# Starting the kv matmuls of batches 3 and 4 one schedule slot later in a fused attention and MLP kernel

## The chip, the cores and the metric

The kernel runs on one core of one Trainium2 chip. The metric is device time in microseconds (us) of the whole program. Executions of a kernel on this core differ by some tenths of a us, sometimes by more than one. Names used below: PE is the tensor engine, PEld its weight loads, DVE the vector engine, ACT the scalar engine, POOL the engine that issues the loads, SP the engine whose queue issues the DMA transposes and the output stores.

## The reference, cut to what matters

```python
def _attn_ref(q, k, v, g_norm):                      # q, k, v: (8, 8, 576, 64)
    kv = np.einsum('bhsd,bhse->bhde', k, v)          # one 64x64 matrix per batch and head
    out = np.einsum('bhsd,bhde->bhse', q, kv)
    rms = np.sqrt(np.mean(out * out, axis=-1, keepdims=True) + 1e-06)
    return out / rms * g_norm

def _moe_ref(x, g_ln, w_ch1, w_ch2):                 # x: (8, 576, 512)
    xn = (x - mean) / sqrt(var + 1e-06) * g_ln
    return x + np.maximum(xn @ w_ch1, 0.0) @ w_ch2   # 512 -> 2048 -> 512
```

## The kernel before

The MLP is the long part: for each batch, `mm1` (x to 2048 columns) and `mm2` (back to 512). The attention of later batches is interleaved with it by hand. A counter ticks once per group of four 512-column matmuls of the MLP (or the same number of columns in smaller pieces), 0.87 us; one such group is a *slot*. `at(slot, fn)` puts a piece of attention at a slot, and within a slot the pieces are emitted in the order of their fractional slot numbers. In the traces each engine runs its own instructions in the order emitted (in e4, e6 and e8 below, the one piece of DVE work whose slot is moved is the one that changes places there).

```python
    def load_batch(b, *after):
        for element in after:
            nc.gpsimd.tensor_copy(gate, element)      # POOL waits here until `element` exists
        load(k_in[b % NB], k, b)
        load(v_in[b % NB], v, b)
        load(q_in[b % NB], q, b)

    def kv_of(b):
        kv_ps = ps_m.tile([128, HP, D], f32, tag="misc", name="kv_ps")
        kvp = held[b] = kv_pack[b % 4]
        ...                                           # 40 matmuls kv_ps <- k_in, v_in
        nc.scalar.copy(kvp[:D, :, :D], kv_ps[:D])
        nc.scalar.copy(kvp[D:, :, D:], kv_ps[D:])

    def turn_q_dma(b):
        q_p = kv_in.tile([128, JJ, H, D], bf16, tag="qp", bufs=2)
        nc.vector.tensor_copy(q_p.rearrange("p j h d -> p h j d"), q_in[b % NB])
        q_t = qt_pool.tile([128, JJ, HP, 128], bf16, tag="qt", name="qt")
        nc.sync.dma_start_transpose(...)              # qt <- q_p, on SP's queue
        qts[b] = q_t
```

A tile of 128 tokens then goes through `o` (PE: qt times kv), a chain of norms on ACT and DVE that ends in `xc`, and a DMA transpose on SP's queue into `xT_blk`, which `mm1` reads. The schedule of batches 3 and up, with the parts that matter here:

```python
    for b in range(3, B):
        s = 32 * b                                    # slot at which mm1 of batch b starts
        at(47 if b == 3 else s - 60,
           lambda b=b: load_batch(b, qts[b - 1][...], ...))
        d = -41 if b == 3 else -45
        at(s + d, lambda b=b: kv_of(b))               # slot 55 for batch 3, slot 83 for batch 4
        at(s + d + 1.7, lambda b=b: turn_q_dma(b))    # 56.7 and 84.7
        for j in range(J):
            o = s + d + (11 if b == 3 else 13) + 5 * j
            plan_tile(o, lambda b=b, j=j: main_tile(b, j), o + 6, False)
        if b % 2:
            plan_tile(s - 14, lambda b=b: rem_tile(b), s - 8, False)
```

`plan_tile(o, ...)` puts the tile's first half (`o`, squares, sums) at slot `o`, its second half (`y`, `x`, `xc` on DVE) at `o + 2`, the variance at `o + 6`, and the DMA transpose at the slot given as the third argument (`o + 6` too for a tile of a batch). The first `o` of batch 3 is at slot 66, that of batch 4 at slot 96. `mm1` of batch 3 starts at slot 96 too, right after that `o`.

## Time and profile before

| | before |
|---|---|
| median of 4 runs | 290.67 us (290.46 to 290.76) |
| span of the profiled execution | 289.9 us |
| PE busy, granted clock | 96%, 0.997 |

Two parts of the page: the busy time of each engine, and the chain of work that ended last, by engine.

```profile
PE 278.9 (96%) x2270; PEld 158.1 (55%) x2295; DVE 149.8 (52%) x331; ACT 153.0 (53%) x333; POOL 41.2 (14%) x69
...
PE 69%; DMA 19%; issue 9%; POOL 2%; DVE 0%; POOLq 0%
```

PE has no free time to speak of, so only a gap on PE can be gained. (The Trainium skill, Perfetto Trace Analysis, section "Identifying the Most-Contended Engine", warns that matmul busy time is not a good measure of the distance to the peak, since matmuls are pipelined. It is used here only to say that PE seldom waits.) There were 2295 weight loads but 2270 matmul records: 25 records are missing.

Of the chain's 19% DMA, the page puts 14% down to the v_in loads. The three waits of PE that are longest in total (us in total, number, longest):

```profile
PE even L225 <- DMA v_in<-in_v_dram: 2.0, 1, 2.0
PE p L198 <- DVE eps_sb L137: 1.2, 1, 1.2
PE kv_ps L246 <- DMA v_in<-in_v_dram: 1.0, 2, 0.6
```

The first two are the start of the program. The third is the kv matmuls waiting for their v. The timeline of PE (start, duration, what; in brackets the idle time before it and what ended it) places them:

```profile
73.14 0.82 PE L246 MATMUL kv_ps<-v_in,k_in 128*64 128x64 bf16 x40 [0.39 <-DMA v_in<-in_v_dram]
74.12 0.59 PE L429 MATMUL p<-w_sb,m 128*128 128x512 bf16 x2 [0.16 <-issue]
...
101.03 0.82 PE L246 MATMUL kv_ps<-v_in,k_in 128*64 128x64 bf16 x40 [0.61 <-DMA v_in<-in_v_dram]
102.00 0.38 PE L429 MATMUL p<-w_sb,m 128*128 128x512 bf16 x1 [0.16 <-issue]
...
113.01 0.39 PE L271 MATMUL o_ps<-kv_pack,qt 128*128 128x128 bf16 x4
113.28 0.59 PE L413 MATMUL p<-xT_blk,w_sb 128*128 128x512 bf16 x2
```

The first lines of the pairs are kv of batch 3 and of batch 4. The last two lines are the first `o` of batch 4 and the first matmul of `mm1` of batch 3; that matmul needs the last xT transpose of batch 3. The timeline of SP's queue shows when it was issued:

```profile
107.51 3.14 SPq L205 DMA_TRANSPOSE qt<-q_p  x1
110.70 1.26 SPq L352 DMA_TRANSPOSE xT_blk<-xc  x1
```

By its semaphore it landed near 113.15, so `mm1` at 113.28 was already on its heels, without a visible wait. In front of it in the queue stands the q transpose of batch 4.

### The profile page before, as it was taken

The numbers are of one execution on the slowest core, as the hardware profiler recorded it, in microseconds if no ns is written. First come the engines' busy times: TensorE is split into PE (matmuls) and PEld (weight loads), VectorE is DVE, ScalarE is ACT, GpSimd is POOL, SyncE is SP. The second block draws the span as 40 slices with busy tenths as digits, with TensorE's granted clock in tenths as the row PEclk, the third lists the DMA queues.
The fourth block names the chain that finished last, engine by engine and source line by source line (L and its number), as shares of the span: only waits on it lengthen the run. The fifth ranks groups of instructions, "written<-read, shape, count | busy, mean of one in ns | idle before, by whom it ended". The sixth has DMA issues, their size and how long they took to land.

```text
span 289.9 us, 5728 instructions
## 1 busy us (share of the span) xinstructions
PE 278.9 (96%) x2270; PEld 158.1 (55%) x2295; DVE 149.8 (52%) x331; ACT 153.0 (53%) x333; POOL 41.2 (14%) x69
## 2 busy tenths in 40 slices
PE   8789999999999999999999999999999999999994
PEld 3579755995479644445444444444444444444444
DVE  5675119937897783765366925762578200220022
ACT  3467844985369732882288418920894076016400
POOL 8432510041006003200500032000000000000000
PEclk9999999999999999999999999999999999999998
DMA  7999999969786959996994189937202410230033
GB/s 213 198 206 203 199 177 193 221 109 192 138 171 98 198 100 169 196 162 110 158 221 77 39 148 215 156 79 158 55 18 58 107 36 0 45 83 20 0 74 74
DMA packets 67546, 36.76 MB, mean 127 GB/s; under 512 B 35516, under 2 KB 62524, under 8 KB 67520
## 3 DMA queue, kind: packets, MB, share of 16 engines
q0 software_dynamic: 28528, 17.76, 43.6%
q1 hardware_dynamic: 38480, 17.91, 30.3%
q10 hardware_dynamic: 512, 0.72, 0.7%
q8 instruction: 18, 0.29, 0.4%
q14 instruction: 8, 0.07, 0.1%
HBM read 36.71 MB, written 9.44 MB: 159 GB/s over the span
## 4 chain that ended last, share of the span: by engine, by line
PE 69%; DMA 19%; issue 9%; POOL 2%; DVE 0%; POOLq 0%
PE p L429 35%; PE p L413 31%; DMA v_in<-in_v_dram 14%; DMA w_sb<-in_moe_w_ch_dram 5%; PE o_ps L271 2%; PE kv_ps L246 1%; POOL k_in L93 0%; POOL v_in L93 0%; POOL k_in L94 0%; POOL q_in L94 0%; DVE o_sb L434 0%; POOL gate L98 0%; POOLq L93 0%; POOLq L94 0%; POOLq L690 0%
## 5 line engine op out<-in xcount | busy, mean ns | idle before, releaser
L413 PE MATMUL p<-xT_blk,w_sb 128*128 128x128 bf16 (+2 forms) x1017 | 131.3, 285 | 0.8
L429 PE MATMUL p<-w_sb,m 128*128 128x512 bf16 (+2 forms) x591 | 126.6, 368 | 1.5 <-issue 1.0
L416 ACT ACTIVATE m<-p 128x512 bf16<-128x512 f32 x144 | 85.4, 595 | 42.8 <-PE p L413 40.4
L413 PEld LDWEIGHTS <-w_sb 128*128 128x128 bf16 x1024 | 78.7, 98 | 44.5 <-issue 1.1
L429 PEld LDWEIGHTS <-m 128*128 128x128 bf16 x608 | 57.0, 98 | 62.1
L434 DVE SCALAR_TENSOR_TENSOR o_sb<-p,rstd,x_blk 128x512 f32<-128x512 f32 (+2 forms) x38 | 27.3, 720 | 52.9 <-PE p L429 47.3
L277 ACT ACTIVATE sq<-o_ps 128x512 f32<-128x512 f32 x35 | 20.9, 596 | 43.5 <-PE o_ps L271 43.5
L298 DVE TENSOR_REDUCE ss<-sq 128x8 f32<-128x512 f32 x35 | 23.7, 679 | 12.8 <-ACT sq L277 12.6
L340 ACT ACTIVATE dev<-x_blk,st_blk 128x512 f32<-128x512 f32 x36 | 25.7, 714 | 5.7 <-DVE st_blk L326 5.7
L332 DVE SCALAR_TENSOR_TENSOR xc<-x_blk,st_blk,g_ln_sb 128x512 bf16<-128x512 f32 x34 | 25.6, 752 | 1.2
L303 DVE TENSOR_TENSOR y<-o_ps,inv 128x512 f32<-128x512 f32 x33 | 22.8, 692 | 3.4 <-PE p L413 0.5
L322 DVE SCALAR_TENSOR_TENSOR x_blk<-y,g_norm_sb 128x512 f32<-128x512 f32 x33 | 22.8, 691 | 1.1
L315 DVE RECIPROCAL inv<-rms 128x8 f32<-128x8 f32 x36 | 7.2, 201 | 22.9 <-ACT rms L308 22.9
L422 DVE RECIPROCAL rstd<-rstd 128x4 f32<-128x4 f32 x9 | 1.6, 175 | 32.1 <-ACT rstd L421 32.0
L308 ACT ACTIVATE rms<-ss,eps_sb 128x8 f32<-128x8 f32 x36 | 10.7, 296 | 10.6 <-DVE ss L298 10.4
L98 POOL COPY gate<-qt 1x1 bf16<-1x1 bf16 x5 | 0.9, 178 | 106.8 <-DMA qt<-q_p 106.8
L271 PEld LDWEIGHTS <-qt 128*128 128x128 bf16 (+1 forms) x156 | 10.3, 100 | 7.5 <-issue 1.7
L271 PE MATMUL o_ps<-kv_pack,qt 128*128 128x128 bf16 (+1 forms) x156 | 13.6, 220 | 0.0
L198 PE MATMUL p<-fill_sb 128*128 128x512 bf16 x26 | 8.1, 461 | 1.3 <-DVE eps_sb L137 1.2
L246 PEld LDWEIGHTS <-k_in 128*64 128x64 bf16 x280 | 5.0, 112 | 3.7 <-issue 3.6
L249 ACT CAST kv_pack<-kv_ps 64x256 bf16<-64x256 f32 x7 | 2.5, 364 | 8.1 <-PE kv_ps L246 8.1
L340 ACT ACTIVATION_READ_ACCUMULATOR dev<-x_blk,st_blk 128x1 f32 x36 | 6.8, 189 | 0.0
(80 smaller groups left out, 110.9 us busy)
## 6 DMA issues: line engine op xcount, KB each, us to landing
out_dram<-o_sb SPq DMA_DIRECT2D x70, 128.0 KB, 2.5
w_sb<-in_moe_w_ch_dram POOLq DMA_DIRECT2D x8, 512.0 KB, 14.7
q_in<-in_q_dram POOLq DMA_DIRECT2D x7, 320.0 KB, 12.1
k_in<-in_k_dram POOLq DMA_DIRECT2D x7, 320.0 KB, 5.8
v_in<-in_v_dram POOLq DMA_DIRECT2D x7, 320.0 KB, 8.6
q_in<-in_q_dram POOLq DMA_DIRECT2D x8, 256.0 KB, 12.0
k_in<-in_k_dram POOLq DMA_DIRECT2D x7, 256.0 KB, 6.7
v_in<-in_v_dram POOLq DMA_DIRECT2D x7, 256.0 KB, 10.0
```

Source lines behind the costliest of these rows:

```text
L271: nc.tensor.matmul(flat[rows, hp * 128:(hp + 1) * 128], lhsT=lhsT_of(hp), rhs=kvp[:, hp, :], start=True, stop=True)
L277: nc.scalar.activation(self.sq_t, self.o_ps, func=AF.Square)
L298: nc.vector.tensor_reduce(self.ss, self.sq_t, axis=AX.X, op=ALU.add)
L303: nc.vector.tensor_mul(self.y_t, self.o_ps, self.inv().to_broadcast([128, H, D]))
L308: nc.scalar.activation(self.r, self.ss, func=AF.Sqrt, scale=1.0 / D, bias=eps_sb)
L322: nc.vector.scalar_tensor_tensor(x_blk[:, ts].rearrange("p (h d) -> p h d", h=H), in0=self.y_t, scalar=1.0, in1=g_norm_sb.to_broadcast([12 ...
L332: nc.vector.scalar_tensor_tensor(self.xc_t, in0=x_blk[:, self.ts], scalar=st[:, 1, self.ts:self.ts + 1], in1=g_ln_sb, op0=ALU.add, op1=ALU ...
L340: nc.scalar.activation(dev, x_blk[:, ts], func=AF.Square, bias=st[:, 1, ts:ts + 1], accum_out=st[:, 2, ts:ts + 1])
L413: nc.tensor.matmul(p1[:, i, :], lhsT=w1_sb[:, kk, de * 128:(de + 1) * 128], rhs=blk[2][:, kk, sl], start=(kk == 0), stop=(kk == nK - 1))
L416: nc.scalar.activation(m1[:, de0:de0 + per, sl], p1, func=AF.Relu)
L429: nc.tensor.matmul(p2[:, c0:c1], lhsT=m1s[b][:, de, ts * 128:(ts + 1) * 128], rhs=w2_sb[:, de, c0:c1], start=(de == 0), stop=(de == nDe - 1))
L434: nc.vector.scalar_tensor_tensor(o_sb[:, c0:c1], in0=p2[:, c0:c1], scalar=rstds[b][:, ts:ts + 1], in1=blks[b][0][:, ts, c0:c1], op0=ALU.mu ...
```

## The change

The intent is to let v land before PE comes to the kv matmuls: they move behind one more slot of MLP matmuls, and PE does that work in the time in which it waited.

```diff
-        at(s + d, lambda b=b: kv_of(b))
+        at(s + d + (1 if b < 5 else 0), lambda b=b: kv_of(b))
```

## The prediction

> **What bounds the kernel.** The tensor engine: the page has PE busy 96% of the 289.9 us span at a granted clock of 0.997, with 69% of the chain that ended last. In the waits of PE, the only wait on data in mid-kernel is kv_ps (the kv matmuls, L246) on the v_in load: 1.0 us, twice. The timeline of PE places them: kv of batch 3 starts at 73.14 after 0.39 us idle, kv of batch 4 at 101.03 after 0.61. kv of batch 5 (130.45) waits for nothing.
>
> **What the change does.** It adds and removes nothing. The 40 kv matmuls of batches 3 and 4, with their two casts on ACT, move behind one more slot of four 512-column matmuls (0.87 us in the timeline). turn_q_dma still comes right after kv, so VectorE and the DMA queue keep their order. The new kv is first used ten slots later.
>
> **Gain at the two places.** From the end of the matmul before to the next one after, an undisturbed kv (batch 5) takes 0.91 us. Batch 3 takes 72.75 to 74.12 = 1.37, batch 4 100.42 to 102.00 = 1.58. So 0.46 and up to 0.67 us can go. v_in of batch 3 landed at 72.96; kv would now start near 73.6: wait gone. v_in of batch 4 landed near 100.85; its load was gated at 89.10 by the last xT transpose of batch 2, which hangs on a VectorE chain that is back to back from 74 to 82, so I don't expect it earlier. PE would reach that kv near 100.42 - 0.46 + 0.87 = 100.83: at most 0.2 us of wait is left. PE is then 0.9 to 1.1 us ahead.
>
> **What takes part of it back.** The first mm1 matmul of batch 3 (113.28) needs all four xT tiles. The last transpose is issued at 110.70 and, by its semaphore, lands near 113.15: that matmul already starts on its heels. (The issue bar ends at 111.96; that the data movement lies outside it is what the Trainium skill, Perfetto Trace Analysis, section "DMA Instruction — HWDGE (DVE, Sync)", says, and this landing agrees.) If PE is 0.9 us early, it waits here, except as far as the transpose comes earlier too. Its chain backwards: qt transpose on the same queue (107.51 to 110.65), q_p copy on VectorE (106.63), VectorE back to back since 96.57, ACT rstd (96.25), ACT back to back since an eviction that waited for PE at 93.47. So it moves with PE as it stands before slot 83: by batch 3's 0.46 us, not by batch 4's gain. PE should get a new wait of about 0.4 us there, and the net gain is about 0.46 us. From there PE is the limit to the end (v_in of batch 5 has 6 us of margin).
>
> **Prediction.** 290.73 - 0.46, say 290.25 us; 8 times in 10 within 289.65 to 290.85. Faster by over 2%: 0.005; within 2%: 0.99; slower by over 2%: 0.005.
>
> **What would show it.** PE's waits: kv_ps on v_in gone or under 0.3 us in total. A new wait of PE at L413 near 112.8, of 0.3 to 0.6 us, released by the xT transpose. rstd on ACT near 95.8, last xT transpose of batch 3 issued near 110.2. kv of batch 5 near 130.0.
>
> **What would make it wrong.** The transpose's chain moves by the full 0.9 us (gain near 1.0), or not at all since ACT or VectorE hold it (gain near 0.05). The load gate of batch 4 shifts, and v_in with it by some tenths. A new buffer wait in mm2 of batch 1, whose last p2 bank has about 0.6 us of margin.

## The result

The time did not move: 290.70 us median (290.36 to 291.18, 4 runs) against 290.67 us, ratio 1.0003, 95% interval 0.9986 to 1.002. (A ratio is the mean time of one kernel's fast runs over that of the other's fast runs of the same rounds, so it is not quite the ratio of the medians.)

The profile after, the page's busy line and all waits of PE:

```profile
PE 282.2 (98%) x2295; PEld 158.1 (55%) x2295; DVE 149.8 (52%) x331; ACT 153.3 (53%) x333; POOL 40.9 (14%) x69
```

```profile
PE p L198 <- DVE eps_sb L137: 1.2, 1, 1.2
PE even L225 <- DMA v_in<-in_v_dram: 0.4, 1, 0.4
PE tp L554 <- DVE xc L547: 0.4, 1, 0.4
PE p L413 <- DMA xT_blk<-xc: 0.2, 1, 0.2
PE kv_ps L246 <- issue: 0.2, 1, 0.2
```

The wait of kv on v_in is gone, and `mm1` waits for the xT transpose. The start of the program also waited 1.6 us less for its first v, by chance. Do not read "PE 98%" as a gain: 25 more matmuls have a record here. The lines of the PE timeline that answer to those before:

```profile
73.11 0.82 PE L246 MATMUL kv_ps<-v_in,k_in 128*64 128x64 bf16 x40
...
100.53 0.82 PE L246 MATMUL kv_ps<-v_in,k_in 128*64 128x64 bf16 x40
...
112.56 1.24 PE L413 MATMUL p<-xT_blk,w_sb 128*128 128x512 bf16 x5 [0.24 <-DMA xT_blk<-xc]
```

Two more waits hide in the weight loads. In the timeline of PEld (the first line is `o` of batch 3, the second `o` of batch 4, both of their first tile):

```profile
83.40 0.23 PEld L271 LDWEIGHTS <-qt 128*128 128x128 bf16 x4 [0.32 <-DMA qt<-q_p]
...
111.92 0.23 PEld L271 LDWEIGHTS <-qt 128*128 128x128 bf16 x4 [0.59 <-DMA qt<-q_p]
```

The view of PE's own waits does not list these two: qt is the weight operand, so the wait belongs to the weight load, and PE's pause in that time lies under the modelled end of the matmul before it. SP's queue after:

```profile
106.83 3.09 SPq L205 DMA_TRANSPOSE qt<-q_p  x1
109.98 1.26 SPq L352 DMA_TRANSPOSE xT_blk<-xc  x1
```

**A measure without the start-up.** From the first matmul to the first kv matmul of batch 2 the profiled executions of all kernels here took 51.7 to 52.7 us, although nothing there was changed. From the first kv matmul of batch 5 to the end they took 159.39 to 159.43 us. So the stretch between, *kv of batch 2 to kv of batch 5*, holds all that the change does: 76.50 us before, 76.20 us after. Times in the rest of the text are counted from the first kv matmul of batch 2.

In that stretch I took, at five places, the distance between the starts of two successive matmuls, less the distance usual at that place (0.31 us in front of kv; 0.11 and 0.22 in front of the first `o` of batches 3 and 4; 0.06 between that `o` and `mm1`). That is the wait there, free of modelled ends. "Sum" is their total, "rest" the stretch less the sum. The table has all runs, those of the next section too.

| run | kv b3 on v_in | o b3 on qt | kv b4 on v_in | o b4 on qt | mm1 b3 on xT | sum | stretch | rest |
|---|---|---|---|---|---|---|---|---|
| before | 0.45 | 0 | 0.68 | 0 | 0.05 | 1.18 | 76.50 | 75.32 |
| after | 0 | 0.20 | 0 | 0.26 | 0.40 | 0.86 | 76.20 | 75.34 |
| e1_after_again | 0 | 0.23 | 0.08 | 0.16 | 0.46 | 0.93 | 76.28 | 75.35 |
| e2_only_batch3 | 0 | 0.20 | 0.62 | 0 | 0.05 | 0.86 | 76.19 | 75.33 |
| e3_only_batch4 | 1.15 | 0 | 0 | 0.26 | 0.40 | 1.81 | 77.14 | 75.33 |
| e4_q4_early | 0 | 0.20 | 0.78 | 0 | 0 | 0.98 | 76.31 | 75.34 |
| e5_kv_far | 0 | 0.21 | 0 | 0.27 | 0.41 | 0.89 | 76.23 | 75.34 |
| e6_kv_far_q4 | 0 | 0.20 | 0 | 0 | 0 | 0.21 | 75.54 | 75.33 |
| e7_kv_far_q4_o3 | 0 | 0 | 0 | 0 | 0 | 0 | 75.32 | 75.32 |
| e8_q4_early_alone | 0.14 | 0.07 | 0.66 | 0 | 0 | 0.88 | 76.21 | 75.34 |

The rest is the same to 0.03 us in all ten, so these five waits are the whole account. The change took away 1.13 us of waiting for v_in and put 0.81 us of waiting for transposes in its place: 0.20 + 0.26 + 0.35 more.

### The profile page after: what moved, and what is told of

The parts are those of the page before. It is cut to its first block, busy times and chain, and to the rows that moved or that the text cites. A ratio compares the mean times of both kernels' runs of the same rounds, so it can differ in the third digit from the quotient of the medians.

```text
span 289.1 us, 5753 instructions
## 1 busy us (share of the span) xinstructions
PE 282.2 (98%) x2295; PEld 158.1 (55%) x2295; DVE 149.8 (52%) x331; ACT 153.3 (53%) x333; POOL 40.9 (14%) x69
## 4 chain that ended last, share of the span: by engine, by line
PE 90%; DMA 3%; DVE 2%; ACT 2%; issue 1%; SPq 1%; DVEq 0%; POOLq 0%
PE p L429 42%; PE p L413 42%; PE o_ps L271 3%; DMA v_in<-in_v_dram 2%; PE kv_ps L246 2%; DMA xT_blk<-xc 1%; ACT m L416 1%; SPq L205 1%; DVE x_blk L289 0%; DVE xc L547 0%; ACT xT_blk L350 0%; PE tp L348 0%; ACT rms L308 0%; DVE ss L513 0%; PE tp L554 0%
## 5 line engine op out<-in xcount | busy, mean ns | idle before, releaser
L413 PE MATMUL p<-xT_blk,w_sb 128*128 128x128 bf16 (+2 forms) x1024 | 131.6, 286 | 0.7 <-DMA xT_blk<-xc 0.2
L429 PE MATMUL p<-w_sb,m 128*128 128x512 bf16 (+2 forms) x608 | 129.1, 368 | 0.0
L413 PEld LDWEIGHTS <-w_sb 128*128 128x128 bf16 x1024 | 78.7, 98 | 44.9 <-issue 1.5
L198 PE MATMUL p<-fill_sb 128*128 128x512 bf16 x27 | 9.2, 498 | 1.2 <-DVE eps_sb L137 1.2
```

What stands on the lines that cost most here:

```text
L413: nc.tensor.matmul(p1[:, i, :], lhsT=w1_sb[:, kk, de * 128:(de + 1) * 128], rhs=blk[2][:, kk, sl], start=(kk == 0), stop=(kk == nK - 1))
L429: nc.tensor.matmul(p2[:, c0:c1], lhsT=m1s[b][:, de, ts * 128:(ts + 1) * 128], rhs=w2_sb[:, de, c0:c1], start=(de == 0), stop=(de == nDe - 1))
```

## The experiments

My theory before these runs (e3 corrects a part of it): PE stands between two limits that move independently of it. v_in lands at a time that PE does not set, and so do the q transpose of batch 3, the q transpose of batch 4, and the xT transpose behind the latter. Taking away the first limit lets PE run into the second. The rivals were that each removed wait is worth its own length, that the gain in the first profile is chance, and that the transposes alone were the limit. The first four runs ran on one chip and share their runs of the kernel before (median 290.74 us); so did the last four (290.68 us).

### The change again, timed more closely

No edit to the changed kernel; 5 rounds.

> The change as it is, timed more closely. The measure used in all these runs, since it leaves out the start-up, which differs from run to run by some 0.4 us: the time from the first kv matmul of batch 2 to the first kv matmul of batch 5 in the trace; 76.50 us before, 76.20 us in the first profile of the change. Theory (gain at the kv waits, given back in part at two transposes: qt of batch 3 at its first o matmul, xT of batch 3 at its first mm1 matmul): 76.2, PE gap of 0.2 to 0.4 in front of mm1 of batch 3, ratio of the times 0.999 (0.3 us). Rival 1, nothing is gained and the profile's 0.30 is chance: 76.5. Rival 2, the recorded prediction, which had only the xT wait: 76.04.

Measured: 290.51 us median (290.42 to 290.77), ratio 0.9992 (0.9978 to 1.0005). Stretch 76.28 us. That is the theory's size, 0.2 us, but the interval of the times still holds no change at all; only the stretch in the trace separates it from the kernel before. The 76.04 is out.

### Each batch alone

```diff
-        at(s + d + (1 if b < 5 else 0), lambda b=b: kv_of(b))
+        at(s + d + (1 if b == 3 else 0), lambda b=b: kv_of(b))     # e2; e3 has b == 4
```

> Only kv of batch 3 one slot later. Theory: its wait of 0.39 goes, about 0.2 of the gain is lost at o of batch 3 waiting for its qt transpose, and the rest is lost at kv of batch 4, which still starts when its v_in lands: a wait of about 0.9 there, first kv matmul of batch 4 at 47.0 to 47.1 as before, batch 5 at 76.4 to 76.5, no change of time. Rival, each removed wait is worth its own length: 76.04, 0.46 us faster.

> Only kv of batch 4 one slot later. Theory: kv of batch 3 still waits 0.4; kv of batch 4 waits for nothing; PE then waits 0.5 to 0.7 in front of mm1 of batch 3 for the xT transpose, whose chain has not moved; batch 5 at 76.4 to 76.5, no change of time. Rival, each removed wait is worth its own length: 75.83, 0.67 us faster.

Measured: 290.67 us (290.43 to 290.78), ratio 0.9995 (0.9982 to 1.0008) for batch 3 alone; 290.57 us (290.40 to 291.43), ratio 0.9993 (0.9978 to 1.0008) for batch 4 alone. Neither is worth anything that shows. The PE timelines, first of e2, then of e3:

```profile
100.06 0.82 PE L246 MATMUL kv_ps<-v_in,k_in 128*64 128x64 bf16 x40 [0.55 <-DMA v_in<-in_v_dram]
```

```profile
72.96 0.82 PE L246 MATMUL kv_ps<-v_in,k_in 128*64 128x64 bf16 x40 [1.08 <-DMA v_in<-in_v_dram]
...
113.05 1.24 PE L413 MATMUL p<-xT_blk,w_sb 128*128 128x512 bf16 x4 [0.23 <-DMA xT_blk<-xc]
```

In e2 the gain of batch 3 is spent at o of batch 3 (0.20) and at kv of batch 4, which starts when v_in lands, as the theory has it. In e3 kv of batch 4 waits for nothing, and PE then waits for two transposes: 0.26 us in front of the first `o` of batch 4 and 0.40 in front of `mm1`.

Both stretches missed the expected 76.4 to 76.5 (76.19 and 77.14). That of e2 alone would not have told the theory from the rival (76.04); its waits do, for the removed 0.45 us came back as 0.20 in front of o, and kv of batch 4 waited as long as before. Both misses begin with one thing: **v_in does not land at a fixed time.** In e2 kv of batch 4 started at 46.77 and not at 47.0 to 47.1, in e3 kv of batch 3 waited 1.15 and not 0.4. In all ten profiles the last v_in load of batch 4 is issued between 38.34 and 38.42, and it lands between 46.60 and 47.66: 8.25 to 9.30 us after its issue. The one of batch 3 takes 7.27 to 9.14 us. So "1.0 us, twice" in one profile is one draw. The transposes are much steadier: q of batch 3 lands at 29.84 to 29.90 in every profile.

In e3 the late v_in is not the whole reason, and there the theory is wrong: **the transposes of batch 4 do not move independently of PE.** The first `o` of batch 3 and SP's queue in e3:

```profile
83.91 0.39 PE L271 MATMUL o_ps<-kv_pack,qt 128*128 128x128 bf16 x4
...
107.33 3.11 SPq L205 DMA_TRANSPOSE qt<-q_p  x1
```

Counted from kv of batch 2, the q transpose of batch 4 was issued at 54.26, against 53.57 before and 53.32 in the changed kernel. In all six profiles that keep DVE's order (before, after, e1, e2, e3, e5) it is issued 23.41 to 23.43 us after the first `o` of batch 3, which itself starts anywhere between 29.89 and 30.84. So it follows PE as it stands at that `o`, and the xT transpose comes behind it. Had both stayed where they were before, PE would have lost next to nothing of the 0.66 us at them and the stretch would have been near 76.5 (an estimate: 77.14 less 0.66), as expected. What does not move with PE is the q transpose of batch 3, and so that `o` cannot start before about 29.9.

### The change, with the transposes of batch 4 issued earlier

The q_p copy of batch 4 stands on DVE behind the second half of the remainder tile, 2.5 us of work. The edit moves that half behind the copy; nothing else on DVE moves, and PE, POOL and SP keep their order. (On ACT one small root moves with it, behind the kv casts.)

```diff
-            plan_tile(s - 14, lambda b=b: rem_tile(b), s - 8, False)
+            plan_tile(s - 14 + (0.8 if b == 3 else 0), lambda b=b: rem_tile(b), s - 8, False)
```

> The change, and the q_p copy of batch 4 ahead of the remainder tile's second half on VectorE (only the order of these moves), so that the qt transpose of batch 4 and the xT transpose queued behind it are issued about 2 us earlier. Theory: the xT transpose is issued near 107.9 instead of 109.98, PE has no gap in front of mm1 of batch 3, batch 5 at 75.8 to 75.9, time 0.998 of before. Rival, that wait stands for something else (the DMA engines are full there, or PE would wait for another thing in its place): 76.2.

Measured: 290.13 us (289.78 to 290.86), ratio 0.998 (0.9965 to 0.9994), the first that is clear of 1. But the profiled execution drew a late v_in, and its PE timeline has this:

```profile
101.16 0.82 PE L246 MATMUL kv_ps<-v_in,k_in 128*64 128x64 bf16 x40 [0.71 <-DMA v_in<-in_v_dram]
```

So its stretch is 76.31 and not 75.85, and since PE came to `mm1` late, the missing wait there proves nothing. The profile neither supports nor refutes the theory; the times favour it. The design was weak: one slot is not enough for a late v_in. The next runs take v_in out of the question first.

### Neither limit, one limit, the other limit

Runs e5, e6 and e8 together with the kernel before are a table of two by two: kv late enough for any landing of v_in (yes or no), q transpose of batch 4 early (yes or no). e7 adds the last wait.

```diff
-        at(s + d + (1 if b < 5 else 0), lambda b=b: kv_of(b))
+        at(s + d + {3: 2, 4: 3}.get(b, 0), lambda b=b: kv_of(b))        # e5, e6, e7
```

```diff
-            plan_tile(s - 14, lambda b=b: rem_tile(b), s - 8, False)
+            plan_tile(s - 14 + (0.8 if b == 3 else 0), lambda b=b: rem_tile(b), s - 8, False)   # e6, e7, e8
```

```diff
-            o = s + d + (11 if b == 3 else 13) + 5 * j
+            o = s + d + (11 if b == 3 else 13) + 5 * j + (1 if b == 3 and j == 0 else 0)        # e7
```

> kv of batch 3 two slots later than before and kv of batch 4 three, so that v_in has landed however late it comes; nothing else. In all profiles so far the time from the first kv matmul of batch 2 to that of batch 5, less the listed waits of PE (kv on v_in, o of batch 3 and of batch 4 on qt, mm1 of batch 3 on xT), is 75.33 to 75.37 us. Theory: no kv wait at all, but the whole gain over the one-slot version is given back at o of batch 4 and mm1 of batch 3, whose qt and xT transposes land at 58.4 and 59.1 whatever PE does: mm1 of batch 3 starts at 59.1 to 59.2, batch 5 at 76.2 to 76.3, waits there 0.6 to 0.8 in sum, time 0.999 of before. Rival, the kv waits are all that binds: 75.35 to 75.55, time 0.997.

> The kernel of the run before, and the q_p copy of batch 4 ahead of the remainder tile's second half on VectorE. Theory: qt of batch 4 and the xT transpose behind it land near 56.7 and 57.5, no wait at o of batch 4 or at mm1 of batch 3; left is 0.2 at o of batch 3; batch 5 at 75.55, time 0.9965 to 0.998 of before, about 0.7 us faster than the run before. Rival, that the transposes are late because the DMA engines are full: no gain over the run before.

> The kernel of the run before, and the first tile of batch 3 (o, and its second half and variance with it) one slot later, so that its qt transpose has landed. Theory: no wait of PE left between batch 2's and batch 5's kv; batch 5 at 75.35, 0.2 us faster than the run before, 0.996 to 0.9975 of before. Rival: the later tile pushes VectorE back, and a new wait appears at xT of batch 3: 75.5 or more.

> The kernel before with only the q_p copy of batch 4 moved ahead, kv where it was. Theory: this lifts a limit that does not bind while kv waits for v_in; kv of batch 3 waits 0.3 to 1.1 and kv of batch 4 0.4 to 1.0, depending on when v_in lands in that execution; no wait at mm1 of batch 3; batch 5 at 76.2 to 77.0, time 0.9985 to 1.0005 of before. Rival, the transposes alone were the limit: 75.7 or less, time 0.998.

Measured:

| | q transpose where it was | q transpose early |
|---|---|---|
| kv where it was | before: 290.68 us (290.43 to 292.03), stretch 76.50 | e8: 290.85 us (290.37 to 291.68), ratio 1.0003 (0.9981 to 1.0024), stretch 76.21 |
| kv far later | e5: 290.63 us (290.36 to 291.11), ratio 0.9992 (0.9973 to 1.001), stretch 76.23 | e6: 289.87 us (289.79 to 290.04), ratio 0.9963 (0.9946 to 0.998), stretch 75.54 |

Each edit alone is worth nothing that the times show, both together 0.8 us of the medians, and no execution of e6 was as slow as the fastest of e5. SP's queue and PE, of e5:

```profile
107.05 3.10 SPq L205 DMA_TRANSPOSE qt<-q_p  x1
110.20 1.27 SPq L352 DMA_TRANSPOSE xT_blk<-xc  x1
```

```profile
112.14 0.40 PE L271 MATMUL o_ps<-kv_pack,qt 128*128 128x128 bf16 x4
112.78 1.46 PE L413 MATMUL p<-xT_blk,w_sb 128*128 128x512 bf16 x6 [0.24 <-DMA xT_blk<-xc]
```

and of e6:

```profile
104.36 3.20 SPq L205 DMA_TRANSPOSE qt<-q_p  x1
107.61 1.26 SPq L352 DMA_TRANSPOSE xT_blk<-xc  x1
```

```profile
111.22 0.39 PE L271 MATMUL o_ps<-kv_pack,qt 128*128 128x128 bf16 x4
111.44 2.75 PE L413 MATMUL p<-xT_blk,w_sb 128*128 128x512 bf16 x11
```

In e5 kv of both batches waits for nothing, two and three slots late, and still `mm1` of batch 3 starts at 59.07, as in the one-slot version (59.04): moving kv further gains nothing, for the two transposes hold PE at the same place. In e6 the q transpose lands 1.96 us earlier and the xT transpose is issued 1.94 us earlier, counted from kv of batch 2 (the lines differ by more, since the start-up of e5 was longer as well), `mm1` follows `o` in 0.22 us without a gap and starts at 58.37. The rival that the DMA engines are full falls: an earlier issue of the q transpose gave an earlier landing. In e8 the queue is as early as in e6, and the wait is at v_in, so the rival that the transposes alone were the limit (75.7 or less) falls too:

```profile
99.79 0.82 PE L246 MATMUL kv_ps<-v_in,k_in 128*64 128x64 bf16 x40 [0.59 <-DMA v_in<-in_v_dram]
```

The 0.29 us by which e8's stretch is shorter than that of the kernel before is a draw: in e8 v_in landed 0.31 us earlier for batch 3 and 0.25 us earlier for batch 4. (The 76.50 of the table is that of the first profile; the times of its cell are those of the runs that e5 to e8 share.)

e7: 290.06 us (289.57 to 290.34), ratio 0.9967 (0.9948 to 0.9986). Its stretch is 75.32 us, 0.22 less than e6, with none of the five waits left, as expected, and no new one at xT. Its times are not better than those of e6. The start-up of its profiled execution was 0.7 us longer than that of e6, and 0.2 us cannot be told in six runs; whether e7 beats e6 stays open. Both are faster than the kernel before by 0.3 to 0.4%, far under 2%.

## Why the prediction was right or wrong

- **Range and class: right, but that says little.** 290.70 lies within 289.65 to 290.85, and "within 2%" is what was measured. The range also holds the time of the kernel before (290.67), so no gain at all falls in it as well as the predicted one; the mechanism is tested by the next points. The point, 290.25, was too low by 0.45 us in the first measurement and 0.26 in the second.
- **"PE's waits: kv_ps on v_in gone or under 0.3 us in total": right** in the first profile (0) and the second (0.08 by the steps).
- **"A new wait of PE at L413 ..., released by the xT transpose": right** in place and cause. The view of waits lists 0.24 us, the steps give 0.40, and the prediction said about 0.4. This wait was found because the landing of that transpose was looked up in the trace, although PE did not wait for it before. (That the move of data lies outside the issue bar is what the Trainium skill, Perfetto Trace Analysis, section "DMA Instruction — HWDGE (DVE, Sync)", says; in the changed kernel the issue bar ended at 111.24 and `mm1` was released at 112.56.)
- **"So it moves with PE as it stands before slot 83: by batch 3's 0.46 us": wrong in size.** The xT transpose was issued 0.30 us earlier (56.76 to 56.46) and 0.25 us in the second profile. The rule itself holds: e3 shows these transposes following PE. The step that failed is that PE would still be 0.46 us ahead at that place. On the way PE met the q transpose of batch 3 at its first `o`, which lands at 29.9 in every profile, and lost 0.20 us: it was 0.25 us ahead from there (`o` at 29.89 instead of 30.15). The prediction used the very fact behind this, the VectorE chain that is back to back from 74 to 82 (the q_p copy of batch 3 stands in it, at 77.51), to say that the load gate would not move, and did not ask what else hangs on it.
- **"A new wait of about 0.4 us there": incomplete.** It was two waits. The first `o` of batch 4 also waited, for its own q transpose, 0.26 us. Net, the prediction has a gain of 0.46 us, the stretch shows 0.30 and 0.22, and of the times only the second measurement shows any, 0.2.
- **"At most 0.2 us of wait is left" at kv of batch 4: right in the changed kernel's two profiles, but not as a bound.** e4, with kv in the same slot, waited 0.78 us. The landing of v_in was taken from one trace as if fixed; it varies by 1.0 us for batch 4 and 1.9 us for batch 3. That the two profiles of the change drew an early enough v_in of batch 4 was luck.
- **"From there PE is the limit to the end": right.** 159.39 to 159.43 us from kv of batch 5 to the end in all ten profiles. (The "6 us of margin" of batch 5's v_in is 3.8 us in the trace, from its landing at 126.68 to kv at 130.45; it was enough.)

What stays open: why v_in's landing varies. All ten profiles have the same issue time to 0.1 us for batch 4 (0.2 us for batch 3); nothing here tells what the loads met on their way.

## What to carry to other kernels

When a wait is to be removed, look up by how much the *next* inputs of the waiting engine are early, also those that show no wait at all, and follow each back to see whether it moves along: the gain is at most the smallest margin of those that do not, not the length of the wait. Here two limits stood close together (`mm1` of batch 3 started at 59.07 in e5, held by the transposes alone from there on, and at 59.05 in e8, held by v_in), so lifting either was worth nothing that the times show, and lifting both 0.8 us; a two by two of edits shows that, and neither edit alone does. Measure such a change by a stretch of the trace that leaves out the start-up, which varies by chance, list the waits inside it, since v_in varies there too, and take a DMA's landing from several profiles before building a slot on it.

## What the Trainium skill lacked or had wrong

- TensorE: Matmul & The Clock Gate, section "Back-to-back issue gap", gives sustained spacings of about 81 ns for 128 columns and 131 ns for 512, and calls its formula N / 2.4 + 2.5 that of a single isolated matmul. In these kernels, streams of weight load and matmul pairs run at 216 ns for 512 columns and 56 ns for 128, at a granted clock of 1.0, and 20 matmuls of 512 columns take 4.32 us in the chain: the isolated formula fits, the sustained figures do not.
- DMA: Bandwidth & Descriptors, section "Issuing engines are not separate DMA queues", says that the sequencer's time to start a DMA is usually small relative to the DMA, and makes no exception there for DMA transposes. For the DMA transposes here it is not: the q transpose holds SP's queue for 3.1 us of the 5.0 us from its issue to its landing, the last xT transpose of batch 3 for 1.3 of about 2.5 us, and in the kernel before, the latter left 0.05 us after the former let go of the queue, though its xc was done at 103.50: the order in that queue decided when `mm1` could start.
- The same page, section "Anatomy of one DMA — SWDGE (gpsimd) path", gives a fit of 2.0 us plus bytes over 436 GB/s and no spread. In ten profiles the last v_in load of batch 4, issued within 0.1 us of the same moment, landed 8.25 to 9.30 us after its issue, that of batch 3 7.27 to 9.14 us. (Other loads were in flight, so this shows the spread that is missing and does not refute the fit for one DMA.)
- Perfetto Trace Analysis has nothing on matmul records that are missing from a trace: 25 of 2295 were missing in the kernel before and none in the changed one, which shows as 3.3 us more of PE busy time and as "issue" gaps of 0.16 us that are not there.
